# Pooled attention and a sine feed-forward on one core: the second layer in 6 units of 768 tokens

## The chip, the core and the metric

The kernel runs on one core of a Trainium2 chip. The metric is device time in microseconds (us), from launch to end; the median of the runs is compared. The core's engines run side by side, each with its own queue in program order: TensorE (PE; its weight loads are PEld), VectorE (DVE), ScalarE (ACT), GpSimd (POOL) and SyncE (SP), which here only issues transfers (DMA). ACT can issue them too. Engines wait for one another by semaphores.

## What is computed

Attention over keys and values pooled by 8, then a two-layer network on the result; all in float32.

```python
k_p, v_p = (t.reshape(B, H, 72, 8, D).mean(axis=3) for t in (k, v))   # B = H = 8, S = 576, D = 64
attn = softmax(q @ k_p.T / 8)
x = heads_side_by_side(attn @ v_p)          # 4608 tokens x 512
h = x @ w_in                                # 512 x 2048
g = h + sin(alpha * h) ** 2 / (alpha + 1e-9)
out = g @ w_out                             # 2048 x 512
```

## The kernel before

Both layers use a scheme of seven products in place of eight for a 2 x 2 block product (Strassen's, in Winograd's form). The first layer runs in 9 units of 512 tokens (`hidden`, products at L848), with the attention of the next batch between its products. Its result g goes to HBM (`g_bridge`) and comes back for the second layer.

The second layer (`outputs`) applies the scheme twice. A unit is 4T tokens, before 4 x 144 = 576, and is loaded as four blocks: r11 and r12 (first half of its tokens; first and second half of the hidden features), r21 and r22 (second half). `outer` makes the operands x5, x6, x7, x3 of the seven outer products from them on VectorE, and `inner` makes four sums s1 to s4 of each operand for its seven inner products. An outer product is one slot k; the slots of a unit, n = 0 to 6, take p in the order 1, 2, 4, 6, 7, 5, 3, so x1 = r11, x2 = r12, x4 = r22 come first. An inner product is 4 matmuls of 128 x 128 weights and T = 144 columns (L1340). The trace has two records for each of these float32 matmuls, so a group `x8` is one inner product.

A slot issues its own inner products 1, 6 and 7 and those numbered 5, 4, 2 and 3 of the slot before. ACT copies partial sums between PSUM halves (L1443, L1468, L1488), and VectorE joins finished outer products into four output blocks (`combine`, buffers ca, cb, cc, cd), turns each block (`out`, L1362, into a buffer o) and stores it with four transfers. All of this stands in the order in which the code records it: no scheduler moves it. SP issues the loads of the next unit (`load_g`, L1286: three at n = 3, r21 at n = 5), the stores of g and the stores of the output, in program order.

For unit 0 r11, r12 and r22 are loaded while the last unit of the first layer runs; r21 is loaded by ACT when that layer has ended. The first products of the second layer stand between the last ones of the first. After the last slot, inner products 5, 4, 2 and 3 remain; the last output block has its second part (4 of 9 blocks of 32 columns) turned and stored by `early`, the first 5 behind the last product.

Of the kernel before, what the change touches and what calls it, by code (L numbers as in the profile page):

```python
# [22 lines left out]
JW = 2  # L23
# [17 lines left out]
class Kernel:  # L41
    def __init__(self, tc, q, k, v, w_in, w_out, alpha, out):
        self.tc, self.nc = tc, tc.nc
        self.q, self.k, self.v = q, k, v
        self.w_in, self.w_out, self.alpha, self.out = w_in, w_out, alpha, out
        self.B, self.H, self.S, self.D = q.shape
        self.Sp = self.S // POOL
        self.DM = self.H * self.D
        self.FF = w_in.shape[1]
        self.K1 = self.DM // P  # L50
        self.K2 = self.FF // P
        self.NP = self.H // 2
# [1224 lines left out]

    def load_g(self, u, names):  # L1280
        for n in names:
            i, j = divmod(("r11", "r12", "r21", "r22").index(n), 2)
            shape = [P, self.NJ, JW, 2, self.T]
            t = (self.gs if n == "r21" else self.gq if n == "r22" else self.gp).tile(shape, F32, name=n)[:]
            t0 = u * self.S + i * 2 * self.T
            (self.nc.scalar if u == 0 and n == "r21" else self.nc.sync).dma_start(out=t.rearrange("p J b i c -> p (J b) (i c)"),  # L1286
                                   in_=self.gd[j, :, :, t0:t0 + 2 * self.T].rearrange("b p c -> p b c"))
            self.R[n] = t

    def outputs(self):  # L1290
# [9 lines left out]
        def outer(u, n):  # L1300
            r = self.R
            if n == 0:
                X[u] = {1: r["r11"], 2: r["r12"], 4: r["r22"]}
                return
            new = lambda p: self.gs.tile([P, self.NJ, JW, 2, T], F32, name=f"x{p}")[:]
            x = X[u]
            if n == 1:
                x[5] = new(5)
                tt(flat(x[5]), flat(r["r21"]), flat(x[4]), OP.add)
            if n == 2:  # L1310
                x[6] = new(6)
                tt(flat(x[6]), flat(x[5]), flat(x[1]), OP.subtract)
            if n == 3:
                x[7] = r["r21"]
                tt(flat(x[7]), flat(x[1]), flat(x[7]), OP.subtract)
            if n == 4:
                x[3] = new(3)
                tt(flat(x[3]), flat(x[2]), flat(x[6]), OP.subtract)

        def inner(u, n):  # L1320

            x = X[u][ORDER[n]]
            e = self.ne
            self.ne = not e
            new = lambda i: (self.gs if e and i > 1 else self.gq).tile([P, self.NJ, T], F32, name=f"s{i}{int(e)}")[:]
# [19 lines left out]

        def early(st):

            t = C[st["u"]]["c"]
            with_z(t, st["yz"])
            add(t[:, :, 1], t[:, :, 1], st["x1"][:])  # L1350
            if st["u"] == self.B - 1:
                out(st["u"], 0, 1, t, 5, queues=both)

        def with_z(t, z):
            add(t[:, 1], t[:, 1], z[:, 1:2, :].to_broadcast([P, 2, T]))

        def out(u, i, j, t, n0=0, n1=2 * T // 32, queues=4 * (nc.sync,)):

            if n0 or n1 * 32 == 2 * T:
                C[u]["o"] = self.op.tile([P, 2 * T // 32, 2, 32], F32, name="o", bufs=3)  # L1360
            o = C[u]["o"]
            nc.vector.transpose(out=o[:, n0:n1].rearrange("p n h c -> p h n c"),  # L1362
                                in_=t[:].rearrange("p h i c -> p h (i c)").rearrange("p h (n c) -> p h n c", c=32)[:, :, n0:n1])
            r = u * self.S + i * 2 * T
            for a in range(4):
                c = j * 2 * P + a * 64
                queues[a].dma_start(out=self.out[r + 32 * n0:r + 32 * n1, c:c + 64].rearrange("(n k) c -> k n c", k=32),
                                        in_=o[32 * a:32 * a + 32, n0:n1].rearrange("k n h c -> k n (h c)"))

        def combine(st):  # L1370

# [6 lines left out]
            if p in (1, 4, 5):  # L1378
# [6 lines left out]
                if p == 5 and u < self.B - 1:  # L1385
                    add(c["a"][:], c["a"][:], t[:])
                    out(u, 1, 1, c["a"])
                    add(c["c"][:], c["c"][:], t[:])
                elif p == 5:
                    nc.gpsimd.tensor_tensor(out=c["c"][:], in0=c["c"][:], in1=t[:], op=OP.add)  # L1390
                    add(c["a"][:], c["a"][:], t[:])
                    later.append(lambda: out(u, 1, 1, c["a"], queues=both))
            elif p == 2:
                o = block("cd")
                with_x(o, c["a"])
                with_z(o, z)
                out(u, 0, 0, o)
# [5 lines left out]
            elif p == 7:  # L1403

                t = c["a"]
                with_x(t, c["c"])
                with_z(t, z)
                add(c["b"][:], c["b"][:], t[:])
                out(u, 1, 0, c["b"])
            else:  # L1410
                t = c["c"]
                add(t[:, :, 0], t[:, :, 0], x[0][:])
                if u < self.B - 1:
                    out(u, 0, 1, t)
                else:
                    out(u, 0, 1, t, 0, 5, both)

        both = 2 * (nc.sync, nc.scalar)
        later = []
        last = None  # L1420
        seq = [(u, n) for u in range(self.B) for n in range(7)]
        outer(0, 0)
        A = {}
        for _ in inner(0, 0):
# [2 lines left out]
        for k in range(len(seq) + 1):  # L1427
            st = None
            if k < len(seq):
                u, n = seq[k]  # L1430
                st = {"u": u, "p": ORDER[n], "A": A.pop((u, n))}
                if 0 < n < 5 and k != 1:
# [5 lines left out]
                if n == 6 and u + 1 < self.B:  # L1438
                    outer(u + 1, 0)
                x0 = st["x0"] = self.bank([P, 2, T])  # L1440
# [34 lines left out]
            if last:  # L1475
                if k != 1:
                    second()
                third()
                if k == 5:
                    self.inner_w(3, self.gs)  # L1480
                combine(last)
            for _ in sums:
                pass
            if k == 1:
# [4 lines left out]
            if later:  # L1489
                later.pop()()  # L1490
            last = st

    def run(self):
        nc, tc = self.nc, self.tc
        pool = lambda s, n, b, **kw: s.enter_context(tc.tile_pool(name=n, bufs=b, **kw))
        with ExitStack() as top:
            const = self.const = pool(top, "const", 1)
            self.tp = pool(top, "tp", 1)
# [6 lines left out]
            engines = {nc.tensor.engine, nc.vector.engine, nc.scalar.engine, nc.gpsimd.engine, nc.sync.engine}  # L1505
            self.wq = pool(top, "wq", 1)
            with ExitStack() as one:
                self.wp = pool(one, "wp", 1)
                self.hp = pool(one, "hp", 2)
                self.xq = pool(one, "xq", 1)  # L1510
# [34 lines left out]
                for u in range(self.NU):  # L1545
# [8 lines left out]
                            x[i].append(lambda: next(w))  # L1554
                    elif u > self.B - 1:
                        homes.close()
                        self.gq = pool(top, "gq", 1, side="right")
# [51 lines left out]
```

## Time and profile before

| | us |
|---|---|
| median of 3 runs (902.22 to 903.03) | 902.47 |
| the profiled execution | 902.87 |
| its span | 901.0 |
| first product of the second layer starts | 506.70 |
| last product of the second layer starts its last group | 895.60 |

A row of the timeline reads: start, duration, engine, line, operation, output <- inputs by the program's names (numbers left out, so r is any of r11 to r22 and x any of x3 to x6), partitions x elements, count, and in brackets the idle time before it and what ended that. A row of the windows reads: the stretch, its length, the busy time and count of PE, PEld, DVE, ACT and POOL, the clock that TensorE was granted, the busy share of the DMA engines, and GB/s. The ends of matmuls are modelled and overlap; their pace is read from start to start.

### The profile page before, as it was taken

The numbers are of one execution on the slowest core, as the hardware profiler recorded it, in microseconds if no ns is written. First come the engines' busy times: TensorE is split into PE (matmuls) and PEld (weight loads), VectorE is DVE, ScalarE is ACT, GpSimd is POOL, SyncE is SP. The second block draws the span as 40 slices with busy tenths as digits, with TensorE's granted clock in tenths as the row PEclk, the third lists the DMA queues.
The fourth block names the chain that finished last, engine by engine and source line by source line (L and its number), as shares of the span: only waits on it lengthen the run. The fifth ranks groups of instructions, "written<-read, shape, count | busy, mean of one in ns | idle before, by whom it ended". The sixth has DMA issues, their size and how long they took to land.

```text
span 901.0 us, 17940 instructions
## 1 busy us (share of the span) xinstructions
PE 894.6 (99%) x7010; PEld 816.3 (91%) x7010; DVE 678.0 (75%) x1010; ACT 447.9 (50%) x1071; POOL 212.5 (24%) x218
## 2 busy tenths in 40 slices
PE   9999999999999999999999999999999999999998
PEld 5787888888888888888888999999999999999997
DVE  7776867768576675764558799979798888889895
ACT  5687776877768777687976611211111111111111
POOL 5698443825337262430000000000000000000000
PEclk9999999999999999999999999999999999999999
DMA  9957957759586585557226346261618172534401
GB/s 264 245 153 206 243 146 210 189 164 253 139 222 184 180 222 145 171 158 282 94 82 223 101 146 191 66 191 35 224 30 230 31 201 64 172 92 127 138 15 40
DMA packets 128371, 141.13 MB, mean 157 GB/s; under 512 B 46416, under 2 KB 95328, under 8 KB 128288
## 3 DMA queue, kind: packets, MB, share of 16 engines
q1 hardware_dynamic: 125504, 137.88, 53.4%
q10 hardware_dynamic: 2784, 2.11, 0.9%
q8 instruction: 56, 0.92, 0.5%
q14 instruction: 27, 0.22, 0.1%
HBM read 75.37 MB, written 47.19 MB: 136 GB/s over the span
## 4 chain that ended last, share of the span: by engine, by line
PE 97%; DVE 2%; DMA 1%; SPq 0%; issue 0%; ACT 0%; DVEq 0%
PE PS L848 46%; PE PS L1340 41%; PE PS L1038 3%; PE PS L317 2%; PE PS L612 2%; PE PS L625 1%; DMA h<-in_v_dram 1%; DVE x L1295 1%; DVE s L1295 0%; DVE r L1295 0%; PE PS L568 0%; PE PS L570 0%; PE PS L289 0%; PE PS L278 0%; PE PS L478 0%; SPq L164 0%
## 5 line engine op out<-in xcount | busy, mean ns | idle before, releaser
L848 PE MATMUL PS<-home,a 128*128 128x256 f32 x1104 | 258.1, 381 | 0.1
L848 PEld LDWEIGHTS PS<-home,a 128*128 128x128 f32 x1104 | 205.3, 190 | 32.3 <-issue 4.6
L848 PE MATMUL PS<-home,as 128*128 128x256 f32 x768 | 182.6, 381 | 0.0
L848 PEld LDWEIGHTS PS<-home,as 128*128 128x128 f32 x768 | 141.8, 190 | 19.7 <-ACT PS L822 1.2
L1390 POOL TENSOR_TENSOR cc<-cc,cb 128x576 f32<-128x576 f32 x1 | 2.0, 1977 | 501.7 <-DVE cb L1295 501.7
L1340 PE MATMUL PS<-s,wb 128*128 128x144 f32 x896 | 119.1, 286 | 0.0
L1340 PEld LDWEIGHTS PS<-s,wb 128*128 128x128 f32 x896 | 113.7, 190 | 0.1
L1015 ACT ACTIVATE s<-s,c 128x256 f32<-128x256 f32 (+1 forms) x228 | 113.5, 565 | 0.0
L821 DVE TENSOR_TENSOR h<-PS,p 128x512 f32<-128x512 f32 x72 | 49.3, 684 | 64.0 <-PE PS L848 37.4
L131 POOL TENSOR_TENSOR kvin<-kvin 96x768 f32<-96x768 f32 (+3 forms) x42 | 73.8, 1756 | 70.3 <-DMA kvin<-in_v_dram 68.1
L1468 ACT COPY PS<-PS 128x144 f32<-128x144 f32 x56 | 14.7, 263 | 145.0 <-PE PS L1340 138.4
L1008 ACT ACTIVATE s<-h,al 128x256 f32<-128x256 f32 x144 | 65.6, 509 | 38.3 <-DVE h L821 38.3
L1340 PE MATMUL PS<-r,wb 128*128 128x144 f32 x512 | 73.3, 286 | 0.3 <-DVE r L1295 0.3
L1340 PE MATMUL PS<-s,a 128*128 128x144 f32 x512 | 73.2, 286 | 0.0
L1008 ACT ACTIVATE s<-PS,al 128x256 f32<-128x256 f32 x144 | 60.2, 471 | 18.8 <-PE PS L848 17.9
L1060 DVE TENSOR_TENSOR h<-PS,s 128x512 f32<-128x512 f32 x36 | 24.8, 689 | 57.4 <-ACT s L1015 57.4
L1340 PEld LDWEIGHTS PS<-r,wb 128*128 128x128 f32 x512 | 67.1, 190 | 0.5 <-DVE r L1295 0.5
L1340 PEld LDWEIGHTS PS<-s,a 128*128 128x128 f32 x512 | 67.1, 190 | 0.0
L822 ACT COPY PS<-PS 128x512 f32<-128x512 f32 x72 | 41.5, 576 | 35.4 <-PE PS L848 30.6
L1488 ACT COPY PS<-PS 128x144 f32<-128x144 f32 x56 | 14.7, 263 | 88.1 <-PE PS L1340 88.1
L1340 PE MATMUL PS<-x,wb 128*128 128x144 f32 x384 | 54.9, 286 | 0.0
L1340 PE MATMUL PS<-s,we 128*128 128x144 f32 x384 | 54.9, 286 | 0.0
(216 smaller groups left out, 1407.5 us busy)
## 6 DMA issues: line engine op xcount, KB each, us to landing
g_bridge<-h SPq DMA_DIRECT2D x72, 512.0 KB
r<-g_bridge SPq DMA_DIRECT2D x31, 1152.0 KB
out_dram<-o SPq DMA_DIRECT2D x122, 72.0 KB
kvin<-in_k_dram SPq DMA_DIRECT2D x14, 576.0 KB
q<-in_q_dram SPq DMA_DIRECT2D x7, 1024.0 KB
kvin<-in_v_dram SPq DMA_DIRECT2D x14, 512.0 KB
aM<-tr SPq DMA_DIRECT2D x54, 92.0 KB
aM<-tr SPq DMA_DIRECT2D x54, 88.0 KB
```

The costliest lines, as they stand in the source:

```text
L131: self.nc.gpsimd.tensor_tensor(out=t[..., 0:w] if w > D else out, in0=t[..., 0:w], in1=t[..., w:2 * w], op=OP.add)
L317: nc.tensor.matmul(ps[e][r0 + r:r0 + r + q.shape[-1], h, :], q[s], kb[s, hp, :], start=True, stop=True)
L612: nc.tensor.matmul(o[r:r + 64], w, x, start=start and i < 2, stop=False, skip_group_check=True)
L821: add = lambda o, x, y: nc.vector.tensor_tensor(out=o, in0=x, in1=y, op=OP.add)
L822: copy = lambda o, x: nc.scalar.copy(out=o, in_=x)
L848: nc.tensor.matmul(ps[:, jj, :], self.A[p][:, kk, f * P:(f + 1) * P], x[:, kk, :], start=(start and n == 0), stop=(kk == 1), skip_group_ch ...
L1008: self.nc.scalar.activation(out=G.s[:, i, jj, j, :], in_=src[:, jj], func=AF.Sin, scale=self.al[:, f:f + 1])
L1015: self.nc.scalar.activation(out=x, in_=x, func=AF.Square, scale=self.c[:, f:f + 1])
L1038: nc.tensor.matmul(o, W[m][:, G.J - J0], X[m], start=start and n == 0, stop=True, skip_group_check=True)
L1060: add = lambda o, x, y: self.nc.vector.tensor_tensor(out=o, in0=x, in1=y, op=OP.add)
L1340: nc.tensor.matmul(out, W[:, J // 2, J % 2, :], A[:, J, :], start=(start and J == 0), stop=(J == self.NJ - 1), skip_group_check=True)
L1468: nc.scalar.copy(out=x1[:, 0, :], in_=x0[:, 1, :])
```

## The change

The second layer runs in 6 units of 768 tokens: T becomes 192, a product has 192 columns, and the loops over `self.B` units run over `self.NO = 6`. Each block of operands grows by a third, so buffers are shared:

- `big` gives the blocks r11 to r22, x5 and x6 their buffers. r12 and x6 change places from unit to unit, r21 and x5 after unit 0; x3 is computed in place of x2. r22 has a pool of its own, opened where the operands of the last first-layer unit lay.
- For unit 0 r11 and r12 are loaded early as before, but r22 when the last product of the first layer has ended, by SP; r21 by ACT as before. The loads of later units are spread over n = 3 to 6, of unit 1 in the order r11, none, r12, r22 with r21.
- `outer` of unit 0 makes x6 = x4 - x1, then adds r21, and makes x5 only in slot 4, x3 in slot 5. Later units do as before.
- The o buffer is single (before three), and cd goes.
- The end: inner product 2 of the last slot goes to one PSUM bank and 3 to another. `early` now also adds what can be added ahead (by POOL, with one ACT copy), turns the full block c["a"] there, and turns and stores the second half of the last block. `half` then finishes each half of the features: the first is added and turned before the last product, the second after it, and then both are stored.

```diff
-        self.T = self.S // 4
+        self.NO = 6
+        self.T = self.B * self.S // (4 * self.NO)
+    def big(self, n, u):
+        if u % 2:
+            n = {"r12": "x6", "x6": "r12"}.get(n, n)
+        if u:
+            n = {"r21": "x5", "x5": "r21"}.get(n, n)
+        return (self.gp if n in ("r11", "r12") else self.gx if n == "r22" else self.gs).tile([P, self.NJ, JW, 2, self.T], F32, name=n)[:]
...
+            if u == 0:
+                if n == 1:
+                    x[6] = self.big("x6", u)
+                    op(x[6], x[4], x[1], OP.subtract)
+                if n == 2:
+                    op(x[6], x[6], r["r21"], OP.add)
+                if n == 3:
+                    x[7], x[5] = self.big("x5", u), r["r21"]
+                    op(x[7], x[1], r["r21"], OP.subtract)
+                if n == 4:
+                    op(x[5], x[5], x[4], OP.add)
...
+            if n == (4 if u else 5):
+                x[3] = x[2]
+                op(x[3], x[2], x[6], OP.subtract)
...
+            t, z = C[st["u"]]["c"], st["yz"]
+            if st["u"] < self.NO - 1:
+                with_z(t, z)
+                add(t[:, :, 1], t[:, :, 1], st["x1"][:])
+                return
+            zc = self.big("r22", st["u"])[:, 0, 0, 0, :]
+            nc.scalar.copy(out=zc, in_=z[:, 1, :])
+            plus(*more.pop())
+            plus(t[:, 1, 0], zc)
+            later.pop()()
+            add(t[:, 1, 1], t[:, 1, 1], z[:, 1, :])
+            add(t[:, :, 1], t[:, :, 1], st["x1"][:])
...
+            turned(o, t, T // 32, 2 * T // 32)
+            stored(st["u"], 0, 1, o, T // 32, 2 * T // 32, both)
+        def half(st, h):
+            t, o = C[st["u"]]["c"], last_o[0]
+            add(t[:, h, 0], t[:, h, 0], st["x0"][:, h])
+            turned(o, t, 0, T // 32, h, h + 1)
+            if h:
+                stored(st["u"], 0, 1, o, 0, T // 32, both)
...
+        def out(u, i, j, t, queues=4 * (nc.sync,)):
+            o = self.op.tile([P, 2 * T // 32, 2, 32], F32, name="o", bufs=1)
...
-                if n == 3 and u + 1 < self.B:
-                    self.load_g(u + 1, ("r11", "r12", "r22"))
-                if n == 5 and u + 1 < self.B:
-                    self.load_g(u + 1, ("r21",))
+                if n > 2 and u + 1 < self.NO:
+                    self.load_g(u + 1, (later_loads if u else first_loads)[n - 3])
...
-                        x[5].append(lambda: self.load_g(0, ("r11", "r12", "r22")))
+                        x[5].append(lambda: self.load_g(0, ("r11", "r12")))
...
+                homes.close()
+                self.gx = pool(top, "gx", 1, side="right")
+                self.load_g(0, ("r22",))
                 self.end_hidden()
```

More of the change, by code (lines that the diff above doesn't have):

```diff
@@ L1282, in load_g @@
             i, j = divmod(("r11", "r12", "r21", "r22").index(n), 2)
-            shape = [P, self.NJ, JW, 2, self.T]
-            t = (self.gs if n == "r21" else self.gq if n == "r22" else self.gp).tile(shape, F32, name=n)[:]
-            t0 = u * self.S + i * 2 * self.T
+            t = self.big(n, u)
+            t0 = u * 4 * self.T + i * 2 * self.T
             (self.nc.scalar if u == 0 and n == "r21" else self.nc.sync).dma_start(out=t.rearrange("p J b i c -> p (J b) (i c)"),
@@ L1302, in outer, with inner @@
             if n == 0:
-                X[u] = {1: r["r11"], 2: r["r12"], 4: r["r22"]}
+                X[u] = {1: r["r11"], 2: r["r12"]}
                 return
[L1305 to L1309, printed above, removed]
-            if n == 2:
[L1311 to L1320, printed above, removed]
+            x, op = X[u], lambda o, a, b, f: tt(flat(o), flat(a), flat(b), f)
+            if u == 0:
[9 more added lines that the diff above has]
+                    op(x[5], x[5], x[4], OP.add)
+            else:
+                if n == 1:
+                    x[5] = self.big("x5", u)
+                    op(x[5], r["r21"], r["r22"], OP.add)
+                if n == 2:
+                    x[6] = self.big("x6", u)
+                    op(x[6], x[5], x[1], OP.subtract)
+                if n == 3:
+                    x[7] = r["r21"]
+                    op(x[7], x[1], x[7], OP.subtract)
+            if n == (4 if u else 5):
+                x[3] = x[2]
+                op(x[3], x[2], x[6], OP.subtract)
+        def inner(u, n):
+            if n == 2:
+                X[u][4] = self.R["r22"]
             x = X[u][ORDER[n]]
@@ L1324, in inner, with new @@
             self.ne = not e
-            new = lambda i: (self.gs if e and i > 1 else self.gq).tile([P, self.NJ, T], F32, name=f"s{i}{int(e)}")[:]
+            def new(i):
+                y = e and not (i == 1 and (u, n) == (0, 1))
+                return (self.gs if y and i else self.gq).tile([P, self.NJ, T], F32, name=f"s{i}{int(y)}")[:]
             s1, s2 = new(0), new(1)
@@ L1384, in combine @@
                 with_z(t, z)
-                if p == 5 and u < self.B - 1:
+                if p == 5 and u < self.NO - 1:
                     add(c["a"][:], c["a"][:], t[:])
@@ L1389, in combine @@
                 elif p == 5:
-                    nc.gpsimd.tensor_tensor(out=c["c"][:], in0=c["c"][:], in1=t[:], op=OP.add)
+                    plus(c["c"][:, :, 1], t[:, :, 1])
+                    more.append((c["c"][:, :, 0], t[:, :, 0]))
                     add(c["a"][:], c["a"][:], t[:])
@@ L1393, in combine @@
             elif p == 2:
-                o = block("cd")
+                o = block("cc")
                 with_x(o, c["a"])
@@ L1412, in combine @@
                 add(t[:, :, 0], t[:, :, 0], x[0][:])
[L1413 to L1416, printed above, removed]
+                out(u, 0, 1, t)
         both = 2 * (nc.sync, nc.scalar)
-        later = []
+        later, more, last_o = [], [], []
         last = None
-        seq = [(u, n) for u in range(self.B) for n in range(7)]
+        seq = [(u, n) for u in range(self.NO) for n in range(7)]
+        first_loads = ("r11",), (), ("r12",), ("r22", "r21")
+        later_loads = ("r11",), ("r22",), ("r12",), ("r21",)
         outer(0, 0)
@@ L1431, in outputs @@
                 st = {"u": u, "p": ORDER[n], "A": A.pop((u, n))}
-                if 0 < n < 5 and k != 1:
+                if 0 < n < 6 and k != 1:
                     outer(u, n)
-                if n == 3 and u + 1 < self.B:
-                    self.load_g(u + 1, ("r11", "r12", "r22"))
-                if n == 5 and u + 1 < self.B:
-                    self.load_g(u + 1, ("r21",))
-                if n == 6 and u + 1 < self.B:
-                    outer(u + 1, 0)
-                x0 = st["x0"] = self.bank([P, 2, T])
+                if n > 2 and u + 1 < self.NO:
+                    self.load_g(u + 1, (later_loads if u else first_loads)[n - 3])
+                if n == 6 and u + 1 < self.NO:
+                    outer(u + 1, 0)
+                if k + 1 < len(seq):
+                    x0 = st["x0"] = self.bank([P, 2, T])
+                else:
+                    i, j = sorted((self.turn + d) % 5 for d in (1, 2))
+                    self.turn = (self.turn + 2) % 5
+                    x0 = st["x0"] = self.PS[:, i:j + 1:j - i, 0:T]
                 yz = st["yz"] = self.abank([P, 2, T])
@@ L1477, in outputs @@
                     second()
+                if not st:
+                    half(last, 0)
                 third()
@@ L1480, in outputs @@
                     self.inner_w(3, self.gs)
-                combine(last)
+                if st:
+                    combine(last)
+                else:
+                    half(last, 1)
             for _ in sums:
```

30 lines of the change are left out of this document (15 added, 15 removed).

## The prediction

> **What bounds the kernel now.** I read the busy shares first, then the chain that ended last, then the stretch around 500 to 540 us and the last 20 us in order of time.
>
> ```profile
> span 901.0 us, 17940 instructions
> PE 894.6 (99%) x7010; PEld 816.3 (91%) x7010; DVE 678.0 (75%) x1010; ACT 447.9 (50%) x1071; POOL 212.5 (24%) x218
> PE 97%; DVE 2%; DMA 1%; SPq 0%; issue 0%; ACT 0%; DVEq 0%
> 535.83 360.92 PE PS L1340 x2944
> 0.00:535.80 535.80, 24.01 (x192) 23.93 (x192) 1.00 0.64 184
> ```
>
> TensorE is busy 99% of the span and 97% of the chain of waits. From 535.83 us to its last product the chain is one piece, 2944 records of the second layer's products (L1340) without a gap. The last row is the busy time of L1340 alone in the first stretch: 192 more records, 3136 in all (8 units x 7 x 7 products x 4 tiles, two records for each matmul). So the cost of the second layer is its number of records times the pace, plus what TensorE waits between 506 and 536 us, plus a tail after its last product. A saving on another engine counts only in those last two.
>
> **The pace.** 360.92 us / 2944 = 122.6 ns for a record of 144 columns. The first layer, with 256 columns, gives a second point:
>
> ```profile
> 461.81 3.62 PE L848 MATMUL PS<-home,a 128*128 128x256 f32 x16
> 465.26 3.62 PE L848 MATMUL PS<-home,as 128*128 128x256 f32 x16
> ```
>
> 16 records from start to start take 3.45 us, 215.6 ns each. The change makes 2352 records (6 x 7 x 7 x 4 x 2) of 192 columns, for which no row exists. On the line through the two points a column costs 93.0 / 112 = 0.830 ns and a record 3 ns beside its columns, so 192 columns take 122.6 + 48 x 0.830 = 162.5 ns. Bounds: at 144 columns' rate (0.851 ns a column) 163.5 ns, at 256 columns' (0.842) 161.7 ns. I take the line. 3136 x 122.6 = 384.5 us becomes 2352 x 162.5 = 382.2 us: **-2.3 us** (bounds +0.1 and -4.2). All that fewer, wider products can save is the 3 ns on 784 records; the arithmetic is the same.
>
> **The junction of the layers.** This is where the gain is at risk. Unit 0 is now loaded in another way: r22 gets a buffer where the last first-layer operands lie, so its load waits for the last L848 product, while before it was loaded with r11 and r12 near 471 us. VectorE needs it soon. The rows of before:
>
> ```profile
> 512.11 1.89 PE L848 MATMUL PS<-home,a 128*128 128x256 f32 x8
> 514.92 0.39 ACTq L1286 DMA_DIRECT2D r<-g_bridge  x1
> 520.01 0.75 DVE L1295 TENSOR_TENSOR s<-r 128x576 f32<-128x576 f32 x1
> 520.79 0.76 DVE L1295 TENSOR_TENSOR s<-s,r 128x576 f32<-128x576 f32 x1
> 521.47 0.75 DVE L1295 TENSOR_TENSOR s<-r 128x576 f32<-128x576 f32 x1
> 522.14 0.45 DVE L1295 TENSOR_TENSOR ca<-ca,PS 128x288 f32<-128x288 f32 x1
> 522.50 0.75 DVE L1295 TENSOR_TENSOR s<-r,s 128x576 f32<-128x576 f32 x1
> 523.17 2.55 DVE L1295 TENSOR_TENSOR x<-r,r 128x2304 f32<-128x2304 f32 x1
> 525.76 2.56 DVE L1295 TENSOR_TENSOR x<-x,r 128x2304 f32<-128x2304 f32 x1
> 528.42 1.05 PEld L1340 LDWEIGHTS PS<-x,wb 128*128 128x128 f32 x8
> 533.23 2.55 DVE L1295 TENSOR_TENSOR r<-r,r 128x2304 f32<-128x2304 f32 x1
> 533.32 2.03 PEld L1340 LDWEIGHTS PS<-s,wb 128*128 128x128 f32 x16
> 535.83 1.03 PEld L1340 LDWEIGHTS PS<-r,wb 128*128 128x128 f32 x8 [0.48 <-DVE r L1295]
> ```
>
> From the first operation on r22 (520.01) to x6 (528.32) VectorE runs 8.3 us without a pause, and TensorE takes x6 at 528.42, just on its cadence: no stall, no slack. The next chain, x6 to x7 (535.78), takes 7.46 us against 56 records x 122.6 = 6.87 us of products, and there TensorE waits: its cadence would have been 533.32 + 16 x 0.1226 = 535.28, so 0.55 us are lost now.
>
> After the change each operation grows with its elements. 576 elements take 752 ns and 2304 take 2553 ns:
>
> ```profile
> L1295 DVE TENSOR_TENSOR s<-r 128x576 f32<-128x576 f32 x64 | 48.1, 752 | 0.8
> L1295 DVE TENSOR_TENSOR x<-r,x 128x2304 f32<-128x2304 f32 x8 | 20.4, 2552 | 0.0
> ```
>
> That is 1.04 ns an element: +0.2 us for 576 to 768, +0.8 for 2304 to 3072, +0.1 for 288 to 384. The chain on r22 (four short sums, one 288, two long; x6 is now (r22 - r11) + r21, still two long ones) becomes 8.3 + 0.8 + 0.1 + 1.6 = 10.8 us. TensorE reaches x6 17 groups of 8 records later by 39.9 ns each: 528.42 + 5.43 = 533.85. So r22 must have landed by 533.85 - 10.85 = 523.0, or TensorE waits for every microsecond beyond.
>
> When does it land? Its load leaves when the last L848 product ends (514.0 above, +0.64 for two longer groups ahead: 514.6). On SP it stands ahead of the last g stores, which wait for VectorE anyway. r21 leaves ACT's queue 0.9 us later (514.92 + 0.64). Each is now 1536 KB instead of 1152. How long one takes alone is seen when unit 1's first load leaves:
>
> ```profile
> 535.84 12.41 SPq L1286 DMA_DIRECT2D r<-g_bridge  x4
> 537.00:538.00 1.00, 1.00 (x10) 1.00 (x9) 1.00 (x2) 0.38 (x1) 0.00 (x0) 1.00 0.88 84
> 539.00:540.00 1.00, 1.00 (x11) 1.00 (x10) 1.00 (x2) 0.00 (x0) 0.00 (x0) 1.00 1.08 392
> 541.00:542.00 1.00, 1.00 (x10) 1.00 (x10) 1.00 (x2) 0.00 (x0) 0.00 (x0) 1.00 0.13 34
> ```
>
> The last column is GB/s: a slow first microsecond, about 390 KB per microsecond, and all of it in by 541.1, 5.3 us after the issue; with a third more bytes 6.3 us. Alone, r22 would be there at 520.9. With r21 beside it at one cap of 390, both (3.15 MB) are in at about 514.6 + 2.3 + 8.1 = 525.0; r22, 0.9 us ahead, at about 524.0. Last of all, behind r21 and the 1 MB of g stores, it would be 527.7. No row shows two such loads at once; I take an even split, 524.0.
>
> The Trainium skill, "DMA: Bandwidth & Descriptors", section "Issuing engines are not separate DMA queues", says that transfers started by different engines run on the same 16 DMA engines and interleave. By it the second queue buys r22 nothing and the sum is the one below; if r22 were served first the sum would be the second case's.
>
> So TensorE waits 1.0 us for x6. Then x6 to x7: 7.46 + 2.1 (four short sums, 288s with 0.3, the turn of 576 with 0.2, one long) = 9.56 us against 56 x 162.5 = 9.10: 0.45 us. Together 1.45 against 0.55: **+0.9 us** (bounds -0.5 with r22 early and x7 on its cadence, +4.6 with r22 last).
>
> What else moves lies under cover. Unit 0 has one long sum more (x5 anew, 3.4 us): by the same addition x5 is ready 7.4 us and x3 15.9 us after x7, their products start 9.1 and 18.3 us after it; without that 2.4 us of slack it would cost up to 1 us. Unit 1's r22 and r21 leave at slot 6, on SP behind the four stores of block p = 7, about 27 us after x7, and are in by 38; VectorE reads them at 39.5. The single o buffer then makes block p = 3's turn wait for stores queued behind those loads, about 2 us; x6 of unit 1 still comes some 1.6 us ahead. In later units x6 has more:
>
> ```profile
> 667.27 2.55 DVE L1295 TENSOR_TENSOR x<-x,r 128x2304 f32<-128x2304 f32 x1
> 673.01 1.05 PEld L1340 LDWEIGHTS PS<-x,wb 128*128 128x128 f32 x8
> ```
>
> 3.2 us between the end of x6 and its first product, and the loads there are spread over slots 3 to 6. I cost all this at nothing; if the cover fails, each microsecond late is one on the end.
>
> **The tail.** After the last product two operations on VectorE and the last four stores remain:
>
> ```profile
> 893.14 1.98 POOL L1390 TENSOR_TENSOR cc<-cc,cb 128x576 f32<-128x576 f32 x1 [501.68 <-DVE cb L1295]
> 895.60 1.14 PE L1340 MATMUL PS<-s,wb 128*128 128x144 f32 x8
> 896.77 0.46 DVE L1295 TENSOR_TENSOR cc<-cc,PS 128x288 f32<-128x288 f32 x1
> 897.26 0.51 DVE L1362 STREAM_TRANSPOSE o<-cc 128x320 f32<-128x320 f32 x1
> 899.00:900.00 1.00, 0.00 (x0) 0.00 (x0) 0.00 (x0) 0.00 (x0) 0.00 (x0) 1.00 0.47 97
> ```
>
> The half that is left is 192 elements in place of 288 and 320: 0.35 + 0.38 us instead of 0.46 + 0.51, -0.24 us. The stores behind it grow from 40 to 48 KB each, some +0.1. Net **-0.1 us** (-0.3 to +0.3). The work put ahead fits: POOL's three additions (384, 384 and 192 elements, by 1.98 us for 576 about 3.3 us) end some 1.5 us before the last product, the full block's turn and store stand a group ahead.
>
> **The sum.** -2.3 + 0.9 - 0.1 = -1.5 us. The profiled execution took 902.87 us (span 901.0 and 1.87 around it), 0.40 above the median of 902.47; off the median, 901.0.
>
> **The rivals.**
> - *r22 is in by 522.5.* For: alone it needs 6.3 us. Against: r21 leaves 0.9 us behind on the same 390 GB/s. No stall for x6 and little for x7: -2.3 - 0.5 - 0.1 = -2.9, 899.6.
> - *Slower: r22 comes last.* r21 and the g stores pass it, at the cap of 390 GB/s, and TensorE stands still before x6 for 4.7 us: -2.3 - 0.1 + 4.6 = +2.2, 904.7. It decides from a landing at 525.5, where the gain is used up. For it: VectorE would be done with all else by about 521 and would wait; against: r22 is issued first.
> - *The wider product saves nothing.* Time goes by columns alone, 163.5 ns: the pace gives +0.1, the junction +0.9: 903.4. For: 0.851 and 0.842 ns a column are close; against: two points already differ in the right direction.
>
> **How the numbers follow.** 0.2% is 1.8 us, about what a measurement of this kernel can tell from no change. Forecast 0.44 (its own range 900.2 to 902.2), r22 early 0.25, r22 last 0.13, no saving by width 0.10, the rest 0.08 for stalls at later units, mostly slower. Faster than 900.7: 0.24 of r22 early and 0.16 of the forecast, 0.40. Slower than 904.3: 0.12 and 0.06, 0.18. Within: 0.42. The range runs from r22 early, less 0.4 for the pace, to the wider product and the start of r22 late: 899.2 to 904.0.
>
> **What would show it.** A long unbroken chain of second-layer records at 162.5 ns: 161.7 or 163.5 moves the end by 2 us. VectorE idle some 3 us before its first sum on r22, put down to a DMA, and TensorE idle about 1 us before x6's first product and under 0.5 before x7's. No TensorE idle after about 545 us. Less than 0.8 us of VectorE after the last product. The prediction is wrong if r22's sums start before 522 or after 525.5, or if any later unit shows TensorE waiting.

## The result, and the profile after

The changed kernel takes 900.53 us (median of 10 runs, 900.12 to 902.1) against 902.53 us of the kernel before on the same chip: a ratio of 0.9977, 95% interval 0.9969 to 0.9986. A second measurement with 11 runs gave 900.37 us, 0.9975 [0.9966, 0.9984]. So it is 2.0 to 2.4 us faster, just over the 0.2% that can be told from no change.

The page and the chain of waits of the changed kernel's first profiled execution:

```profile
span 900.3 us, 16079 instructions
PE 894.1 (99%) x6226; PEld 815.4 (91%) x6226; DVE 669.5 (74%) x905; ACT 441.2 (49%) x1018; POOL 215.5 (24%) x220
PE 96%; DVE 2%; DMA 1%; issue 0%; ACTq 0%; ACT 0%; DVEq 0%
516.01 8.18 DMA r<-g_bridge
544.79 351.28 PE PS L1364 x2160
```

TensorE is still the bound. Its unbroken chain starts later than before, 544.79 instead of 535.83, and has 2160 records of 162.6 ns instead of 2944 of 122.6. What is new in the chain is r22's load.

This execution took 902.1 us, the longest of its ten. It is not compared by its span, because it lost time ahead of the change. The first second-layer product of this execution and of the second profile of the same kernel:

```profile
508.04 1.46 PE L1364 MATMUL PS<-r,wb 128*128 128x192 f32 x8
```

```profile
506.12 1.46 PE L1364 MATMUL PS<-r,wb 128*128 128x192 f32 x8
```

Before it was 506.70. So I read two stretches in every profile: from the first product of the second layer to the end of the last (390.04 us before, 388.02 and 387.95 after), and the tail from there to the end of the span (4.30 before, 4.26 and 4.27 after). The gain is 2.1 us, nearly all of it inside the second layer; the tail gave 0.04.

The junction in the first profile after, in order of time:

```profile
516.01 0.36 SPq L1294 DMA_DIRECT2D r<-g_bridge  x1
516.89 0.39 ACTq L1294 DMA_DIRECT2D r<-g_bridge  x1
...
524.28 0.96 DVE L1303 TENSOR_TENSOR s<-r 128x768 f32<-128x768 f32 x1 [1.82 <-DMA r<-g_bridge]
...
531.81 3.36 DVE L1303 TENSOR_TENSOR x<-x,r 128x3072 f32<-128x3072 f32 x1
532.55 2.63 PEld L1364 LDWEIGHTS PS<-s,wb 128*128 128x128 f32 x16
535.22 1.27 PEld L1364 LDWEIGHTS PS<-x,wb 128*128 128x128 f32 x8
...
541.38 3.35 DVE L1303 TENSOR_TENSOR x<-r,r 128x3072 f32<-128x3072 f32 x1
541.67 2.63 PEld L1364 LDWEIGHTS PS<-s,wb 128*128 128x128 f32 x16
544.78 1.27 PEld L1364 LDWEIGHTS PS<-x,wb 128*128 128x128 f32 x8 [0.49 <-DVE x L1303]
```

VectorE waits 1.82 us for r22. x6 is taken at 535.22, where the cadence of 16 records would have been 532.55 + 2.60 = 535.15: it comes 0.07 us late. x7's product waits 0.5 us, as before. Behind 545 us TensorE never waits. In the second profile x6 has no gap at all and x7 one of 0.43 us.

The tail, where two halves of 192 elements stand in place of one block of 288 and 320:

```profile
894.59 1.46 PE L1364 MATMUL PS<-s,wb 128*128 128x192 f32 x8
894.86 0.35 DVE L1303 TENSOR_TENSOR cc<-cc,PS 128x192 f32<-128x192 f32 x1 [0.20 <-PE PS L1364]
895.25 0.38 DVE L1407 STREAM_TRANSPOSE r<-cc 128x192 f32<-128x192 f32 x1
896.16 0.35 DVE L1303 TENSOR_TENSOR cc<-cc,PS 128x192 f32<-128x192 f32 x1 [0.53 <-PE PS L1364]
896.55 0.38 DVE L1407 STREAM_TRANSPOSE r<-cc 128x192 f32<-128x192 f32 x1
```

The first half lies under the last product, the second behind it.

### The profile page after: what moved, and what is told of

It reads as the page before. It is cut to its first block, busy times and chain, and to the rows that moved or that the text cites. A ratio compares the mean times of both kernels' runs of the same rounds, so it can differ in the third digit from the quotient of the medians.

```text
span 900.3 us, 16079 instructions
## 1 busy us (share of the span) xinstructions
PE 894.1 (99%) x6226; PEld 815.4 (91%) x6226; DVE 669.5 (74%) x905; ACT 441.2 (49%) x1018; POOL 215.5 (24%) x220
## 4 chain that ended last, share of the span: by engine, by line
PE 96%; DVE 2%; DMA 1%; issue 0%; ACTq 0%; ACT 0%; DVEq 0%
PE PS L849 46%; PE PS L1364 39%; PE PS L1039 3%; PE PS L318 2%; PE PS L613 2%; DVE x L1303 1%; DMA r<-g_bridge 1%; PE PS L626 1%; DVE s L1303 1%; DMA q<-in_q_dram 0%; PE PS L425 0%; PE PS L403 0%; PE PS L571 0%; PE PS L290 0%; PE PS L279 0%
## 5 line engine op out<-in xcount | busy, mean ns | idle before, releaser
L1399 POOL TENSOR_TENSOR cc<-cc,cb 128x384 f32<-128x384 f32 x2 | 2.7, 1383 | 498.1 <-DVE cb L1303 498.1
L1364 PE MATMUL PS<-s,wb 128*128 128x192 f32 x672 | 116.2, 326 | 0.0
L1364 PEld LDWEIGHTS PS<-s,wb 128*128 128x128 f32 x672 | 110.4, 190 | 0.1
L1524 ACT COPY PS<-PS 128x192 f32<-128x192 f32 x42 | 12.7, 303 | 145.2 <-PE PS L1364 133.4
L1364 PE MATMUL PS<-r,wb 128*128 128x192 f32 x432 | 79.0, 326 | 0.0
L1364 PEld LDWEIGHTS PS<-r,wb 128*128 128x128 f32 x432 | 71.7, 190 | 0.1
L1364 PE MATMUL PS<-s,a 128*128 128x192 f32 x384 | 70.2, 326 | 0.0
L1364 PEld LDWEIGHTS PS<-s,a 128*128 128x128 f32 x384 | 63.7, 190 | 0.0
L1549 ACT COPY PS<-PS 128x192 f32<-128x192 f32 x42 | 12.7, 303 | 89.4 <-PE PS L1364 89.4
L1303 DVE TENSOR_TENSOR s<-r 128x768 f32<-128x768 f32 x54 | 51.4, 952 | 5.2 <-PE PS L1364 2.8
L1061 DVE TENSOR_TENSOR h<-h,s 128x1024 f32<-128x1024 f32 x36 | 53.7, 1492 | 1.1 <-ACT s L1016 0.9
```

What stands on the lines that cost most here:

```text
L1061: add = lambda o, x, y: self.nc.vector.tensor_tensor(out=o, in0=x, in1=y, op=OP.add)
L1303: tt = lambda o, x, y, op: nc.vector.tensor_tensor(out=o, in0=x, in1=y, op=op)
L1364: nc.tensor.matmul(out, W[:, J // 2, J % 2, :], A[:, J, :], start=(start and J == 0), stop=(J == self.NJ - 1), skip_group_check=True)
```

## The experiments

Each of the twelve kernels was timed against the kernel before on its chip. "Stretch" is first to last product of the second layer, "stalls" what TensorE's weight loads waited in it, both from the one profiled execution; "tail" is the rest of its span.

| kernel | median us | ratio to before, interval | stretch us | stalls us | tail us |
|---|---|---|---|---|---|
| before | 902.5 to 902.8 | | 390.04 | 0.48 | 4.30 |
| after_again | 900.37 | 0.9975 [0.9966, 0.9984] | 387.95 | 0.43 | 4.27 |
| x7_first | 899.98 | 0.9967 [0.9955, 0.998] | 387.54 | 0 | 4.26 |
| r21_behind | 899.89 | 0.9968 [0.9955, 0.998] | 387.54 | 0 | 4.26 |
| both | 900.03 | 0.9972 [0.9962, 0.9983] | 387.54 | 0 | 4.27 |
| u0_plain | 901.41 | 0.9987 [0.9978, 0.9996] | 388.70 | 1.21 | 4.26 |
| whole_tail | 900.65 | 0.9979 [0.9971, 0.9988] | 387.90 | 0.39 | 4.66 |
| r22_last | 907.75 | 1.0059 [1.0045, 1.0072] | 394.95 | 5.81 | 4.27 |
| units9 | 916.1 | 1.0151 [1.0137, 1.0165] | 403.27 | 3.50 | 4.55 |
| units9_spread | 914.29 | 1.0129 [1.0113, 1.0144] | 401.55 | 1.85 | 4.53 |
| units8 | 906.34 | 1.004 [1.0027, 1.0054] | 393.14 | 3.18 | 4.10 |
| units8_spread | 904.31 | 1.0018 [1.001, 1.0027] | 391.91 | 2.00 | 4.09 |
| units8_plain | 902.67 | 1.0003 [0.9994, 1.0012] | 390.75 | 1.14 | 4.09 |

**The change again.**

> The changed kernel once more, unaltered, as the base of the three kernels beside it. Its records of 192 columns should again take 162.6 ns, the first and the last product of the second layer should stand 388.0 us apart (390.0 in the kernel before), and the time should be 2.0 us below the kernel before. If the 1.3 us by which its first second-layer product came later in its first profile belongs to the change, it shows again; if it is chance of that execution, the first product stands near 506.7 us.

The late first product was chance of that execution: here it stands at 506.12. The pace and the stretch came as expected; the time is 2.4 us below the kernel before instead of 2.0, with an interval of 1.4 to 3.1.

**Where x7's stall comes from.** x7 needs r21 and r11 alone, so it can be formed ahead of the turn of the unit's first output block.

```diff
             elif p == 2:
                 o = block("cc")
...
+                if u == 0:
+                    outer(0, 3)
                 out(u, 0, 0, o)
...
-                if 0 < n < 6 and k != 1:
+                if 0 < n < 6 and k not in (1, 3):
```

> In the first unit x7 is formed ahead of the turn of the first layer's last block, where r21 alone is needed. Theory (TensorE runs without a gap from its first second-layer product to its last but for x6's 0.07 us and x7's 0.5 us): the stall at x7 goes, 0.5 us less than the changed kernel between first and last product (387.5), and x6 is not later. Rival (VectorE as a whole sets this stretch: what is put ahead of the turn comes off x6): the sum put ahead pushes the turn, x5 and x6 by 3.4 us, the stall moves to x6 and the time is 0.5 to 3 us higher than the changed kernel's.

The stretch is 387.54 and no weight load of TensorE waits any more: the theory holds.

**Whether r21 delays r22.**

```diff
-            (self.nc.scalar if u == 0 and n == "r21" else self.nc.sync).dma_start(
+            self.nc.sync.dma_start(
```

> r21 of the first unit is issued on SyncE behind r22 and the stores, not on ScalarE 0.9 us after r22. Theory (r22 landed at 524.28 because it shared its last 2.5 us with r21): r22 lands about 1 us earlier, VectorE's wait for it shrinks from 1.8 to about 0.8 us, x6 is about 1 us earlier; r21, first read at 531.8, lands by 531 still and the time is the same within 0.3 us. Rival (r21 comes last): it is issued near 521, lands near 530 to 532, the sum that reads it waits, and the time is 0.5 to 2 us higher.

The timeline of this run:

```profile
514.80 0.36 SPq L1294 DMA_DIRECT2D r<-g_bridge  x1
...
520.51 0.76 SPq L1294 DMA_DIRECT2D r<-g_bridge  x1
...
521.82 0.96 DVE L1303 TENSOR_TENSOR s<-r 128x768 f32<-128x768 f32 x1 [0.57 <-DMA r<-g_bridge]
...
533.94 1.33 PEld L1364 LDWEIGHTS PS<-x,wb 128*128 128x128 f32 x8
...
543.04 1.33 PEld L1364 LDWEIGHTS PS<-x,wb 128*128 128x128 f32 x8
```

The wait for r22 fell from 1.8 to 0.57 us, as expected, and r21 was in time. That the time would stay the same within 0.3 us was wrong by 0.1 us (stretch 0.41 us shorter): VectorE, 1.2 us ahead, is early for x6 and for x7 too, and x7's stall is gone. So x7's stall belongs to a VectorE that reaches x6 with no time to spare. From x6 to x7 its work takes about 0.45 us longer than TensorE's products, and a VectorE that starts that part just in time for x6 ends it 0.45 late for x7.

**Both together.**

> x7 formed ahead of the turn, and r21 issued behind the stores, together. Each alone brought the stretch from the first to the last product of the second layer from 387.95 to 387.55 us. Theory (what each took away is the same gap on TensorE, 0.43 us at x7): together 387.5 us, and the time that of either alone, 900.0. Rival (each removes a gap of its own): 387.1 us and 0.4 us less than either.

387.54 and 900.03 us: the same gap is taken away twice. These three are versions a little faster than the change. The traces say by 0.4 us; the intervals of the medians overlap that of the changed kernel, so the times alone don't settle it.

**The order of the first unit's sums.**

```diff
         if u:
-            n = {"r21": "x5", "x5": "r21"}.get(n, n)
...
-            if u == 0:
-                if n == 1:
-                    x[6] = self.big("x6", u)
-                    op(x[6], x[4], x[1], OP.subtract)
...
+            if n == 1:
+                x[5] = self.big("x5", u)
+                op(x[5], r["r21"], x[4] if u == 0 else r["r22"], OP.add)
+            if n == 2:
+                x[6] = self.big("x6", u)
+                op(x[6], x[5], x[1], OP.subtract)
...
-                    self.load_g(u + 1, (later_loads if u else first_loads)[n - 3])
+                    self.load_g(u + 1, later_loads[n - 3])
```

> The first unit's sums are formed in the order of all later units: x5 = r21 + x4 at once, x6 = x5 - x1, so that one long sum of 3.4 us fewer runs, but r21 is read by the first of them instead of the second. Theory (r21 landed near 529.0 in the changed kernel, 0.6 us after the time at which that first sum started): x5 waits about 0.6 us, x6 stalls by 0.6 to 0.9 us, x7 comes without a stall, and the time is the changed kernel's plus 0.1 to 0.4 us. Rival (r21 is in by 528): no wait, the stall at x7 vanishes with the sum that is saved, 0.5 us less.

```profile
527.52 3.36 DVE L1301 TENSOR_TENSOR x<-r,r 128x3072 f32<-128x3072 f32 x1 [0.82 <-DMA r<-g_bridge]
...
534.32 1.27 PEld L1350 LDWEIGHTS PS<-x,wb 128*128 128x128 f32 x8 [0.72 <-DVE x L1301]
...
543.89 1.27 PEld L1350 LDWEIGHTS PS<-r,wb 128*128 128x128 f32 x8 [0.49 <-DVE r L1301]
```

The edit also spreads the loads of unit 1 as those of later units. x5 waited 0.82 us for r21 and x6 stalled by 0.72, as the theory said. But x7's 0.49 stayed, so the stretch is 0.75 us longer than the changed kernel's, over the 0.1 to 0.4 expected. The long sum that is saved comes behind x7, so it can't help it; a late x6 delays TensorE and VectorE alike, and x7 is 0.45 late again.

**The last block whole.**

```diff
+        def whole(st):
+            t, o = C[st["u"]]["c"], last_o[0]
+            add(t[:, :, 0], t[:, :, 0], st["x0"][:])
+            turned(o, t, 0, T // 32)
+            stored(st["u"], 0, 1, o, 0, T // 32, both)
...
-                if not st:
-                    half(last, 0)
...
-                    half(last, 1)
+                    whole(last)
```

> The last block of the outputs isn't split: its columns are added whole and turned whole after the last product (0.55 and 0.58 us in place of 0.35 and 0.38 us), with all its stores behind that. Theory (VectorE's two steps after the last product are on the path to the end): 0.3 to 0.5 us between the last product's end and the end of the span above the changed kernel's 4.25 us, and as much in the time. Rival (the end is set by the stores' landing however the sum is split): within 0.1 us of the changed kernel.

The last product and the two operations after it in this run:

```profile
892.40 1.46 PE L1364 MATMUL PS<-s,wb 128*128 128x192 f32 x8
...
893.97 0.56 DVE L1303 TENSOR_TENSOR cc<-cc,PS 128x384 f32<-128x384 f32 x1 [1.50 <-PE PS L1364]
894.56 0.58 DVE L1414 STREAM_TRANSPOSE r<-cc 128x384 f32<-128x384 f32 x1
```

The tail is 4.66 us instead of 4.27. So the split is worth 0.4 us: it pays back what the larger last block would cost (4.66 against the 4.30 of the kernel before), and hardly more. The traces alone say so; the median, 900.65, is above those of the changed kernel (900.37 and 900.53) by less than the intervals allow to tell.

**r22 behind the stores.** The load of the first unit's r22 is recorded after `end_hidden` instead of ahead of it.

```diff
-                self.load_g(0, ("r22",))
                 self.end_hidden()
+                self.load_g(0, ("r22",))
```

> r22 of the first unit is issued behind the stores of the first layer's last block, so about 5 us later, beside r21. Measured from the first product of the second layer, r22 landed 16.2 us after it in the changed kernel. Theory (r22 landed just at the time from which it decides): it lands about 5 to 6 us later, VectorE waits 6 to 8 us for it instead of 1.8, x6 stalls by 4 to 6 us, and the time is 4 to 6 us above the changed kernel, 2 to 4 us above the kernel before. Rival (the products already queued on TensorE give slack): under 1 us above the changed kernel.

```profile
520.22 0.83 SPq L1294 DMA_DIRECT2D r<-g_bridge  x1
...
529.72 0.96 DVE L1303 TENSOR_TENSOR s<-r 128x768 f32<-128x768 f32 x1 [8.76 <-DMA r<-g_bridge]
529.74 2.23 PEld L1364 LDWEIGHTS PS<-r,wb 128*128 128x128 f32 x8 [5.15 <-issue]
529.77 2.71 PE L1364 MATMUL PS<-r,wb 128*128 128x192 f32 x8 [4.88 <-DMA r<-g_bridge]
...
534.12 1.46 PE L1364 MATMUL PS<-r,we 128*128 128x192 f32 x8
```

Its windows (stretch, length, busy time of PE, PEld, DVE, ACT and POOL, granted clock, DMA share, GB/s):

```profile
528.00:529.70 1.70, 0.00 (x0) 0.00 (x0) 0.00 (x0) 0.00 (x0) 0.00 (x0) 1.00 0.15 55
529.70:530.70 1.00, 0.93 (x4) 0.96 (x5) 0.96 (x1) 0.00 (x0) 0.00 (x0) 0.63 0.00 0
530.70:531.70 1.00, 1.00 (x5) 1.00 (x4) 0.91 (x2) 0.00 (x0) 0.00 (x0) 0.50 0.00 0
532.70:533.20 0.50, 0.50 (x3) 0.50 (x2) 0.50 (x2) 0.28 (x1) 0.00 (x0) 0.50 0.16 33
533.70:534.20 0.50, 0.50 (x5) 0.50 (x4) 0.50 (x2) 0.00 (x0) 0.00 (x0) 1.00 0.00 0
```

The theory holds against slack: the stretch is 7.0 us longer than the changed kernel's, even more than the 4 to 6 expected. TensorE stood 4.88 us, and for a product that reads r22 itself, ahead of x6. Then the granted clock was 0.50 until about 533.4, and the first 16 records took 4.35 us (529.77 to 534.12; the row of the second 8 is left out) instead of 2.60: 1.75 us more.

**Narrower units.** 9 units of 128 columns:

```diff
-        self.NO = 6
+        self.NO = 9
```

> The second layer in 9 units of 512 tokens, 128 columns per pass, all else as in the changed kernel: 9 x 7 x 56 = 3528 records. Theory (each record costs 0.830 ns per column and 3 ns of its own, by the line through 144 and 256 columns): 109.3 ns a record, 385.6 us in all, 3.1 us above the changed kernel's 382.5. Rival (columns alone count): 0 to 0.3 us above. Second rival (a weight load of 128 columns bounds the record): over 112 ns a record and over 12 us above. A stall of x6 or x7 may come to it, and is read apart.

Its chain has 2944 records in 329.03 us, 111.8 ns each: 2.5 ns over the line, +11.8 us for 3528 of them against the changed kernel. That is the size that the second rival named (112 ns, 12 us), but whether the weight load is what bounds these records, no run shows. Another 3 us are stalls in the first two units.

**8 units**, the same edit with 8, were meant to leave only the split last block.

> The changed kernel with 8 units of 576 tokens and 144 columns per pass as before, so that of the change only the split last block and its order are left. Theory (the whole gain comes from the wider pass): its records take 122.6 ns again, first to last product of the second layer is 390.0 us as before, and the halves take 0.1 to 0.2 us off the 4.25 us behind the last product: 902.4, 0.1 to 0.2 us below the kernel before. Rival (the halves carry part of the gain by themselves): 0.5 us or more below the kernel before.

Both sides missed: the tail is 0.2 us shorter, as the theory said, but the stretch is 3.1 us longer than before.

```profile
522.86 0.70 ACT L1436 COPY ca<-PS 128x288 f32<-128x288 f32 x2 [3.14 <-DMA g_bridge<-h]
523.80 1.03 PEld L1364 LDWEIGHTS PS<-r,we 128*128 128x128 f32 x8 [0.73 <-ACT PS L1549]
529.83 1.03 PEld L1364 LDWEIGHTS PS<-x,wb 128*128 128x128 f32 x8 [1.08 <-DVE x L1303]
537.29 1.03 PEld L1364 LDWEIGHTS PS<-x,wb 128*128 128x128 f32 x8 [0.55 <-DVE x L1303]
```

ScalarE's first copy into the block ca waits for a store of the first layer: with smaller tiles ca comes to lie where that layer's h was. TensorE's next product waits for ScalarE, and x6 comes late. r22's load also leaves earlier here, at 507.10 instead of 514.10 in after_again. To take this away, the next two kernels give each tile the room of its 192-column form:

```diff
+    def wide(self, pool, name, **d):
+        n = 1
+        for v in d.values():
+            n *= v
+        t = pool.tile([P, n * 192 // self.T], F32, name=name)[:, 0:n]
...
-            return self.op.tile([P, 2, 2, T], F32, name=n)
+            return self.wide(self.op, n, h=2, i=2, c=T)
...
```

> The kernel with 8 units and the split last block once more, with every tile of the second layer given the room of its 192-column form, so that the tiles lie as in the changed kernel. In the run without this, the copy into ca stood 3.1 us for a store of the first layer's last block, and TensorE stood still for 0.73, 1.08, 0.55, 0.27 and 0.55 us in the first two units. Theory (where ca lies made that loss): the copy waits under 1 us, the first two stalls vanish and the others shrink, 390.0 to 390.8 us from the first to the last product of the second layer, and 902.3 to 903.0 in all. Rival (the changed order of the first unit's sums, with one long sum more, costs this at 144 columns): 1.5 to 3 us of stalls remain, 904 to 906.

> The kernel with 9 units of 128 columns, tiles laid out as in the changed kernel. Its record took 111.8 ns. Theory (that is the pace of 128 columns): again 111.8 ns and 11.8 us above the changed kernel for pace alone, and the 3.5 us of stalls in the first two units fall below 1.5 us: 912.5 to 914. Rival (the pace itself came from the layout): 109.3 ns, 904 to 906.

The stalls in units8_spread and the chain of units9_spread:

```profile
528.40 1.03 PEld L1372 LDWEIGHTS PS<-x,wb 128*128 128x128 f32 x8 [0.19 <-DVE x L1311]
535.87 1.03 PEld L1372 LDWEIGHTS PS<-x,wb 128*128 128x128 f32 x8 [0.55 <-DVE x L1311]
...
573.87 1.03 PEld L1372 LDWEIGHTS PS<-s,a 128*128 128x128 f32 x8 [0.71 <-issue]
585.44 1.03 PEld L1372 LDWEIGHTS PS<-x,wb 128*128 128x128 f32 x8 [0.55 <-DVE x L1311]
```

```profile
578.92 329.02 PE PS L1372 x2944
```

At 9 units the pace is again 111.8 ns, so it belongs to the 128 columns; the time, 914.29, is 0.3 over the range of the theory, and 1.85 us of stalls are left where under 1.5 were expected. At 8 units the result lies between the two: the places of the tiles made 1.2 us of the loss, and 2.0 us of stalls remain. For these I took away the long sum that the new order of the first unit adds, with the edit of u0_plain, which also moves one load of unit 1: r22 goes from slot 6 to slot 4, and r21 alone stays in slot 6:

> 8 units, split last block and the tiles laid out as in the changed kernel, as in the run before, but the first unit's sums in the order of all later units, one long sum of 2.55 us fewer. r21's packets ended at 521.5 us there, 1.7 us before x5's start. Theory (that sum is what made VectorE late in the first two units): of the 2.0 us of stalls at most 0.7 is left, 390.0 to 390.6 us from the first to the last product of the second layer, 902.4 to 903.0 in all. Rival (the stalls come from something else in the change, such as where the loads stand): over 1.5 us of stalls remain, 904 and more.

Again between: the stretch falls by 1.16 us to 390.75, the stalls to 1.14 (x6 0.59, x7 0.55), those of the second unit are gone. The time is that of the kernel before. So the first unit's new order, with the loads that go with it, is a good half of the loss. Which of the two it is, the sum or the loads, this run doesn't show. Two rows speak for a part of the loads, the rival that the expectation named. They are the turn of the first unit's last output block (p = 3), in units8_spread and in units8_plain:

```profile
568.40 0.78 DVE L1415 STREAM_TRANSPOSE o<-cc 128x576 f32<-128x576 f32 x1 [2.91 <-DMA out_dram<-o]
```

```profile
563.67 0.78 DVE L1401 STREAM_TRANSPOSE o<-cc 128x576 f32<-128x576 f32 x1
```

In units8_spread VectorE stands for 2.91 us there, longer than the long sum takes, until stores have left the single o buffer. These stores stand on SP behind both loads of slot 6 (issued at 557.94 and 558.52), and the second unit's first stall follows 5.5 us later. In units8_plain slot 6 has one load, and this turn doesn't wait.

The 0.66 us of stalls that are left against the kernel before were not traced further.

## Why the prediction was right

The prediction was 901.0 us, and 900.4 to 900.5 came. Its sum was -2.3 (pace) +0.9 (junction) -0.1 (tail) = -1.5; measured it is -2.0, 0.0 and 0.0. The path it named, pace as the gain and r22's landing as the risk, is the one that the traces show. That the total is only half a microsecond off is in part luck: the junction's cost was put 0.9 too high and the gain of the pace 0.3 too high, and the two errors work against each other.

**The pace** is confirmed, a little smaller. A record takes 162.63 ns where the line through 144 and 256 columns gave 162.5; 3136 x 122.6 = 384.5 becomes 2352 x 162.63 = 382.5 us, -2.0. The rival that width saves nothing (163.5 ns) is out. The line has a lower end: 128 columns take 111.8 ns, not 109.3.

The Trainium skill, "TensorE: Matmul & The Clock Gate", section "Back-to-back issue gap", gives the isolated gap as columns / 2.4 + 2.5 ns. With two cycles for each column of these float32 records, an assumption, that is 162.5 ns at 192 columns, where the trace has 162.6, and 109.2 at 128, where it has 111.8. The same section says that at small widths this formula under-counts, since weight loads share the spacing; no run here isolates weight loads.

**The junction** is the term that was mis-sized: +0.9 was forecast, that is 1.0 us for x6 and 0.45 for x7 less the 0.55 lost before, and 0.0 came, from 0.07 and 0.49 (0 and 0.43 in the second profile) against 0.55 before. The failing step is "No row shows two such loads at once; I take an even split, 524.0". Counted from the first product of the second layer that is 17.3 us, and the break-even of 523.0 is 16.3. VectorE could start on r22 at 16.2 us in both profiles: just even. That the landing fell so near to the break-even is luck as well. It lies closer to the rival "r22 is in by 522.5" (15.8 us) than to the forecast. The break-even itself was right: 1.2 us earlier gains only x7's stall (r21_behind), and 7.0 us later lengthens the stretch by 7.0 (r22_last).

The split was not even because r21 began late. First and last packet of the two loads in the packet records of the traces, beside the issue:

```
kernel        r22: issued  packets            r21: issued  packets
before                                             514.92  515.96 to 520.73
after               516.01  517.04 to 523.62       516.89  521.06 to 529.06
after_again         514.10  515.13 to 521.64       514.98  518.94 to 527.01
r21_behind          514.80  515.83 to 521.25       520.51  523.75 to 528.79
r22_last            520.22  523.72 to 529.17       515.39  516.46 to 521.69
```

Each load that is alone on the way begins 1.0 to 1.1 us after its issue. The two that stand on SP behind the g stores (r21 in r21_behind, r22 in r22_last) begin 3.2 and 3.5 us after theirs, and the packets of those stores last until 524.29 in both. ACT's queue by itself isn't what makes r21 late in the changed kernel, since on it too r21 begins 1.1 us after its issue where it is alone (r22_last). r21 beside r22 begins 4.2 and 4.0 us after its own, when r22 has only 2.6 to 2.7 us left to share. The prediction had both share from the start. Its sign for this step, VectorE idle some 3 us ahead of r22 and TensorE 1 us ahead of x6, came out as 1.8 and 0.1.

The Trainium skill, "DMA: Bandwidth & Descriptors", section "Issuing engines are not separate DMA queues", which the prediction weighed, says that transfers of different engines interleave. The trace agrees for the last 2.6 us of r22's packets, and not for the 4.0 us before them.

**x7** was right to 0.06 us: 0.45 forecast, 0.39 to 0.49 in every run of 192 columns in which x6 came without time to spare.

**The tail** is -0.04 instead of -0.1. VectorE's two operations shrank by the 0.24 us that was worked out. But the first of them starts 0.11 us behind the product's modelled end, before 0.03, and what follows the second takes 3.38 us, before 3.26; that second part is the 0.1 that was put down for the larger stores.

**The rivals.** r22 in by 522.5 would have brought 899.6; without any stall x7_first, r21_behind and both measure 899.9 to 900.0, since the pace gives 2.0 and not 2.3. r22 last was priced at 904.7 and measures 907.75: its landing was put at 527.7, 21.0 us after the first product, and came 23.2 after it; then the pause lowered TensorE's clock, which the prediction left out.

**Under cover.** Two rows of the changed kernel's first profile:

```profile
571.81 0.49 SPq L1294 DMA_DIRECT2D r<-g_bridge  x1
...
584.63 0.98 DVE L1407 STREAM_TRANSPOSE o<-cc 128x768 f32<-128x768 f32 x1 [2.72 <-DMA out_dram<-o]
```

Unit 1's r22 left 27.0 us after x7's product began, as worked out (27). The o buffer's wait was 2.7 us instead of 2, and TensorE never waited behind 545 us. But "I cost all this at nothing", for the extra long sum and the place of the loads, holds only at 192 columns: at 144 the new order and its loads together cost 1.16 us (units8_spread against units8_plain), while at 192 they gain 0.75 (u0_plain against the change), where r21 lands too late to be read first.

So the change is more than a wider product. With the tiles laid out alike, 8 units of 144 columns take 391.91 us for the stretch and 6 of 192 take 387.95. Of these 3.96 us the pace makes 2.0 and the stalls 1.6 (2.00 to 0.43); 0.4 is left without a cause. The wider unit pays for the stalls that the rest of the change would bring; by which operations it does so was not tried.

## What to carry to other kernels

Where one engine is the bound, price a change of tile size by its pace per record (two widths give the line, and the line may end below some width), and then look for the few places where a load has to land on time: work out the break-even there, since here 1.2 us early were worth 0.4 us (r21_behind) and a microsecond late counts in full, or more than in full once the pause is long enough for the clock to fall. A parameter tried alone in a changed kernel (8 units in place of 6) can carry a cost of its own, such as a tile that now lies on a buffer still being stored; read its waits before drawing a conclusion. And an order of sums and loads that suits one size may cost at another.

## What the runs showed of the hardware

- **A second load that began late.** r21's packets began 4.0 and 4.2 us after its issue in the two profiles of the changed kernel, when r22 had been issued 0.9 us earlier by another engine, and 1.0 to 1.1 us after it when no other such load was under way. With 1152 KB (units8_spread) it was 4.0 us too, issued at 514.64 and begun at 518.65. Why, no run here tells.
- **A pause that costs more than itself.** After TensorE had stood for 4.88 us its granted clock was 0.50 for about 3.4 us, and 16 records took 1.75 us longer. The stalls of 0.2 to 1.2 us in the other runs left the granted clock at 1.00. The Trainium skill, "TensorE: Matmul & The Clock Gate", section "What's actually happening", says that the clock falls to half after an idle window of about 3.4 us and comes back after as long a busy one; the trace agrees with the second number (3.4 us at 0.50), and for the first it shows only that 4.88 us are enough and 1.2 us (units9) are not.
